# Blocks of three q tiles, products of ones and a shifted conversion table in a linear attention, MLP and MoE kernel

## The chip, the cores and the metric

The kernel runs on one core of a Trainium2 chip. The metric is device time in microseconds for one execution of the whole program, which computes an attention, an MLP and a mixture of experts one after the other.

## The reference

Cut to what is computed:

```python
# attention: q, k, v are (4, 8, 576, 64), float32
q_s = exp(q - max(q, -1)); q_s /= sum(q_s, -1) + 1e-9      # softmax over the head dimension
k_s = exp(k - max(k, 2));  k_s /= sum(k_s, 2) + 1e-9       # softmax over the sequence
out = q_s @ (k_s^T v)                                       # 2304 tokens x 512
# MLP: 512 -> 2048 -> 512
h = x @ w_in;  x = maximum(0.01 * h, h) @ w_out
# MoE: 8 experts of 512 -> 1024 -> 512, all computed, weighted by P
P = exp(x @ w_gate - max);  8 times: rows to 1, columns to 1, times N / E
out = sum_e P[:, e] * (maximum(x @ w1[e], 0) @ w2[e])
```

## The kernel before

Tokens are taken in six blocks of 384, each of three tiles of 128 tokens. The attention and the MLP are written by hand as a table of half-steps (`at(t, task)` in `plan`, run by `half_step`). Negative half-steps, -13 to -1, hold attention work alone. From half-step 0 on, the MLP runs: step s issues its first product (`first`, tile ph) and at half-step 2s + 1 its second (`second`, tiles y). The MLP's hidden units come in four phases of 24 steps; phase 0 takes blocks 0 to 2 in two passes and then block 3 (steps 12 to 15), block 4 (16 to 19) and block 5 (20 to 23). Tasks are generators: every `yield` hands over to the next half-step, and a task that has yielded PE_NEXT runs after the MLP product of its half-step instead of ahead of it. Each engine executes its instructions in the order in which this table emits them, so an instruction that waits holds all that stand behind it on its engine.

- `q_task` (line 283) makes the softmax of one tile of q in place in `acc`, a stage in each half-step: the maximum on VectorE (L291), the subtraction on GpSimd (L293), the exponential on ScalarE (L295), then sum, add and reciprocal on VectorE (L297 to L299) and the scaling on GpSimd (L300); two half-steps later come four transposes on TensorE (tile pq) and the copy back (L306).
- `k_task` (line 251) does the same for a pair of heads of k (tiles knm, ksm), with transposes (pk, L265), copies (ke, L267) and the product with v (pkv), whose two halves are scaled into `kv` (L281).
- `x_task` (line 308) multiplies the three q tiles of a block by `kv` (px), and splits the result into a rounded part (L331, ScalarE) and a rest (L332, VectorE), both in `xs`. The MLP's `first` of that block reads `xs`.
- `prep_half` (line 138) turns half a unit of the MLP's weights, loaded as 64-bit numbers (tile raw), into two float32r parts: the absolute value on ScalarE (L146), three VectorE operations a half-step later (L148, L149, L152), then the cast on ScalarE (L156) with two more on VectorE (L157, L158), and last two operations (L162, L163), on VectorE for phase 0 (tile wa) and on GpSimd for later phases. Its last stage also issues the load of another raw tile.
- PSUM banks: `bank` takes them in rotation from `spare`. Ahead of the MLP that is the pool ps_m (four buffers) and the four banks y0 to y3, which later hold the MLP's sums; line 758 adds them.
- Line 746 writes `WARM` products of ones into y0 at the start of the program.

```python
755:        (q_load, 0, 2, 3), (v_load, 0, 3), (load,), (load,),
758:    spare.extend((ps_y, f"y{i}") for i in range(4))
759:    for t in range(-R, 0):
760:        half_step(t)
729:    for t, (f, half) in zip((26, 28, 29, 32, 34, 36, 40, 42), halves):
730:        at(t, prep_half, PU + f, half)
```

Of the kernel before, what the change touches and what calls it, by code (L numbers as in the profile page):

```python
# [8 lines left out]
F32 = mybir.dt.float32  # L9
# [3 lines left out]
ALU = mybir.AluOpType  # L13
AX = mybir.AxisListType

P = 128
# [6 lines left out]
def kernel(  # L23
# [26 lines left out]
    nc = tc.nc  # L50
    B, _, HP, S = kt.shape
    NT, DM = out.shape
# [3 lines left out]
    KC = DM // P  # L56
    D = 64
    H = DM // D
    SC = vt.shape[3] // P
    TT = NT // P  # L60
    BLK = 384
    TB = BLK // P
# [15 lines left out]
    ps_y = ctx.enter_context(tc.tile_pool(name="ps_y", bufs=1, space=bass.MemoryType.PSUM))  # L78
# [1 line left out]
    att_ctx, ml_ctx = ExitStack(), ExitStack()  # L80
    later = {}
    PE_NEXT, DONE = 1, 2
    WARM = 10
    FAR = 14

    def r32(ap):
# [3 lines left out]
    ident = const.tile([P, P], F32, name="ident")  # L90
    ones = const.tile([P, P], F32, name="ones")
# [3 lines left out]
    acc = [const.tile([P, XS], F32, name=f"acc{b}") for b in range(NB)]  # L95
# [12 lines left out]
    att = att_ctx.enter_context(tc.tile_pool(name="att", bufs=2, side="right"))  # L108
# [14 lines left out]
    halves = ((0, 0), (1, 0), (0, 1), (2, 0), (1, 1), (3, 0), (2, 1), (3, 1))  # L123
# [57 lines left out]
    spare = [(ps_m, "m")]  # L181

    def bank(name):
        pool, tag = spare[0]
        spare.append(spare.pop(0))
        return pool.tile([P, 512], F32, tag=tag, name=name)

    def mm(o, a, b, start, stop, **more):
        nc.tensor.matmul(o, a, b, start=start, stop=stop, **more)  # L189

    def first(s):
        _, b, u, _, _ = steps[s]
        assert all(("x", i) in ready for i in range(b * TB, (b + 1) * TB)), (s, b)
        assert (u, 0) in ready, (s, u)
        p = bank(f"ph{s}")[:, :BLK]
        wh, wl = unit(u)[:, 0, 0, :], unit(u)[:, 0, 1, :]
        xh, xl = xb(b, 0), xb(b, 1)
        for c in range(KC):
            cs = slice(c * P, (c + 1) * P)
            mm(p, wh[:, cs], xh[:, c, :], c == 0, False)  # L200
            mm(p, wh[:, cs], xl[:, c, :], False, False)
            mm(p, wl[:, cs], xh[:, c, :], False, c == KC - 1)
        hh = h_t[s] = hp_.tile([P, 2, BLK], F32R, tag="hh", name=f"hh{s}")
        g = hp_.tile([P, BLK], F32, tag="g", name=f"g{s}", bufs=1)
        nc.scalar.activation(hh[:, 0, :], p, AF.Prelu, alpha=0.01)  # L205
        nc.scalar.activation(g, p, AF.Prelu, alpha=0.01)  # L206
        nc.vector.tensor_tensor(hh[:, 1, :], g, r32(hh[:, 0, :]), op=ALU.subtract)  # L207
# [72 lines left out]
            js = slice(j * D, (j + 1) * D)  # L280
            nc.scalar.mul(kv[b % 2][js, hp, js], pt[js, js], sm[js])  # L281

    def q_task(i):

        bl = i // TB
        o = i * P - bl * BLK
        qt = acc[bl][:, o * KC : (o + P) * KC]
        qs = qt.rearrange("p (h d) -> p h d", d=D)
        mx = att.tile([P, H, 1], F32, tag="qmx", name=f"qmx{i}", bufs=3)
        sm = att.tile([P, H, 1], F32, tag="qsm", name=f"qsm{i}", bufs=3)  # L290
        nc.vector.tensor_reduce(mx, qs, axis=AX.X, op=ALU.max)  # L291
        yield
        nc.gpsimd.tensor_tensor(qs, qs, mx.to_broadcast([P, H, D]), op=ALU.subtract)  # L293
        yield
        nc.scalar.activation(qt, qt, AF.Exp)  # L295
        yield
        nc.vector.tensor_reduce(sm, qs, axis=AX.X, op=ALU.add)  # L297
        nc.vector.tensor_scalar_add(sm, sm, EPS)
        nc.vector.reciprocal(sm, sm)  # L299
        nc.gpsimd.tensor_tensor(qs, qs, sm.to_broadcast([P, H, D]), op=ALU.mult)  # L300
        yield
        yield PE_NEXT
        pt = bank(f"pq{i}").rearrange("p (c t) -> p c t", t=P)
        for c in range(KC):
            nc.tensor.transpose(pt[:, c, :], qt[:, c * P : (c + 1) * P], ident)
        nc.scalar.copy(qt.rearrange("p (c t) -> p c t", t=P), pt)  # L306

    def x_task(bl):

# [340 lines left out]
    def at(t, f, *a):  # L650
        plan.setdefault(t, []).append((f, a))

    def advance(tasks):
        for task in tasks:
            task[1] = next(task[0], DONE)

    def half_step(t, f=None, *a):
        for g, b in plan.pop(t, ()):
            task = g(*b)
            if task is not None:  # L660
                active.append([task, None])
        now = [x for x in active if x[1] != PE_NEXT]
        then = [x for x in active if x[1] == PE_NEXT]
        advance(now)
        if f is not None:
            f(*a)
        advance(reversed(then))
        active[:] = [x for x in active if x[1] != DONE]
# [34 lines left out]
    for b, tk, tv, ts in (  # L703
# [5 lines left out]
        for hp, t in enumerate(ts):  # L709
# [1 line left out]
                at(tk[hp], k_load, b, hp)  # L711
                at(tv[hp], v_load, b, hp)
            at(t, k_task, b, hp)
    for b, tq, ts in (
        (0, None, (-12, -10, -9)), (1, -12, (-8, -7, -6)), (2, -7, (-3, -3, -2)),
        (3, 2, (8, 9, 11)), (4, 8, (13, 14, 15)), (5, 11, (16, 17, 18)),
    ):
        if tq is not None:
            at(tq, q_load, b, 0, TB)
        for j, t in enumerate(ts):  # L720
            at(t, q_task, b * TB + j)
        at(ts[-1] + 5, x_task, b)
    for t, (u, half) in zip((-12, -8, -5, -1, 3, 6, 8, 11), halves0):
        at(t, prep_half, u, half)
    at(24, lambda: nc.sync.dma_start(wg_t, wg) and None)
    at(26, open_units)
    H2 = 2 * SP

    for t, (f, half) in zip((26, 28, 29, 32, 34, 36, 40, 42), halves):
        at(t, prep_half, PU + f, half)  # L730
    for ph in range(1, NPH - 1):
        for n, (f, half) in enumerate(halves):
# [10 lines left out]

    nc.vector.memset(ones, 1.0)
    nc.scalar.activation(mrow, ones[:, :1], AF.Exp)
    warm = ps_y.tile([P, 512], F32, tag="y0", name="warm")
    for _ in range(WARM):
        mm(warm[:, :P], ones, ones, True, True)
    make_identity(nc, ident)
    for t in kv:  # L750
        nc.gpsimd.memset(t, 0.0)
    for f, *a in (
# [2 lines left out]
        (q_load, 0, 2, 3), (v_load, 0, 3), (load,), (load,),  # L755
    ):
        f(*a)
    spare.extend((ps_y, f"y{i}") for i in range(4))
    for t in range(-R, 0):
        half_step(t)  # L760
    spare[:] = [(ps_m, "m")]
    first(0)

# [9 lines left out]
    t = END  # L773
# [47 lines left out]
```

## Time and profile before

| | us |
|---|---|
| median of 3 runs | 2021.68 (2020.82 to 2025.1) |
| the profiled execution's own time | 2021.46 |
| its span, first to last instruction | 2019.6 |
| TensorE busy | 1990.9 (99%) |
| VectorE busy | 1300.8 (64%) |
| ScalarE busy | 806.7 (40%) |
| GpSimd busy | 486.5 (24%) |

The span is what the profile sees between the first and the last instruction; the execution's own time lies 1.9 us above it. Busy shares are means over stages with different limits: the MoE, which takes most of the span, is a chain of TensorE products, while the first 48 us hold attention work alone. TensorE runs at one of two clocks, 1.2 or 2.4 GHz; the profile gives the granted clock as 0.50 or 1.00.

### The profile page before, as it was taken

To read this page: it belongs to the slowest core of one execution; us is meant where nothing else is said; L and a number is where in the kernel's file an instruction comes from. 1 tells how busy PE (TensorE), PEld (TensorE's weight loads), DVE (VectorE), ACT (ScalarE), POOL (GpSimd) and SP (SyncE) were. 2 spreads that over 40 slices of the span, in tenths; PEclk is the share of its full clock that TensorE was granted. 3 is DMA by queue.
4 is the path that set the end of the run, shared out by engine and by line. 5 is a ranking of instruction groups with operands and counts; after the bars stand their busy time and mean duration, and the time that the engine had idled before them with its cause. 6 is when DMAs were issued, how large, how long until landed. Compare 5 with 4: busy or idle time off the path is not lost.

```text
span 2019.6 us, 26345 instructions
## 1 busy us (share of the span) xinstructions
PE 1990.9 (99%) x10323; PEld 1825.1 (90%) x10323; DVE 1300.8 (64%) x1953; ACT 806.7 (40%) x1367; POOL 486.5 (24%) x476
## 2 busy tenths in 40 slices
PE   7999999999999999999999999999999999999998
PEld 6999999999889999989999999999999999999997
DVE  7766435445786666666766666666686666666663
ACT  6654323234443333333444333334344333333331
POOL 3124222300223223122122231231322322313220
PEclk7999999999999999999999999999999999999999
DMA  6502111100212212212132122121212221211210
GB/s 221 175 12 81 45 43 42 53 1 1 85 43 84 84 42 84 70 56 84 42 115 84 43 84 73 54 84 48 78 68 89 84 82 44 84 55 72 84 42 32
DMA packets 65453, 138.56 MB, mean 69 GB/s; under 512 B 4656, under 2 KB 4656, under 8 KB 65328
## 3 DMA queue, kind: packets, MB, share of 16 engines
q1 hardware_dynamic: 65328, 136.87, 19.6%
q8 instruction: 81, 1.33, 0.3%
q14 instruction: 44, 0.36, 0.1%
HBM read 132.14 MB, written 4.72 MB: 68 GB/s over the span
## 4 chain that ended last, share of the span: by engine, by line
PE 73%; DVE 1%; ACT 0%; issue 0%; ACTq 0%; DVEq 0%
PE e L189 38%; PE pa L189 10%; PE pc L189 10%; PE pd L189 10%; PE pb L189 5%; DVE wa L458 0%; PE y L189 0%; DVE xs L565 0%; ACT wa L457 0%; DVE pm L399 0%; DVE cs L400 0%; PE pcs L189 0%; PE pt L189 0%; PE pg L189 0%; DVE rs L398 0%; DVE rs L396 0%
## 5 line engine op out<-in xcount | busy, mean ns | idle before, releaser
L189 PE MATMUL e<-wb_t,xs 128*128 128x512 f32 x3456 | 803.4, 390 | 0.0
L189 PEld LDWEIGHTS e<-wb_t,xs 128*128 128x128 f32 x3456 | 647.0, 188 | 131.2
L464 POOL TENSOR_TENSOR s<-pair 128x256 f32<-128x256 f32 x96 | 72.5, 755 | 1186.1 <-DMA pair<-in_w 719.3
L558 DVE SCALAR_TENSOR_TENSOR acc<-e,pm,acc 128x512 f32<-128x512 f32 x264 | 193.0, 743 | 99.5 <-PE e L189 98.3
L189 PE MATMUL pa<-xs,wa 128*128 128x384 f32 x1152 | 234.2, 337 | 0.0
L565 DVE SCALAR_TENSOR_TENSOR xs<-c,xs 128x384 fp32r<-128x384 f32 (+1 forms) x192 | 185.2, 983 | 70.9 <-ACT xs L564 70.9
L189 PE MATMUL pc<-xs,wa 128*128 128x384 f32 x1152 | 230.8, 334 | 0.0
L189 PE MATMUL pd<-xs,wa 128*128 128x384 f32 x1152 | 230.6, 334 | 0.0
L564 ACT ACTIVATE xs<-c 128x768 fp32r<-128x768 f32 x192 | 126.8, 682 | 231.8 <-PE e L189 211.1
L189 PEld LDWEIGHTS pa<-xs,wa 128*128 128x128 f32 x1152 | 204.6, 188 | 7.2
L189 PEld LDWEIGHTS pc<-xs,wa 128*128 128x128 f32 x1152 | 202.4, 188 | 0.2 <-issue 0.2
L189 PEld LDWEIGHTS pd<-xs,wa 128*128 128x128 f32 x1152 | 202.4, 188 | 0.1
L207 DVE TENSOR_TENSOR hh<-g,hh 128x384 fp32r<-128x384 f32 x96 | 58.4, 609 | 197.8 <-ACT g L206 197.8
L458 DVE TENSOR_TENSOR wa<-s,wa 128x768 fp32r<-128x768 f32 x96 | 91.8, 957 | 106.1 <-ACT wa L457 106.0
L457 ACT CAST wa<-s 128x768 fp32r<-128x768 f32 x96 | 80.2, 836 | 170.8 <-POOL s L467 150.2
L580 DVE TENSOR_TENSOR c<-c 128x384 f32<-128x384 f32 x96 | 53.9, 561 | 133.4 <-ACT c L600 133.4
L590 ACT COPY c<-pa 128x384 f32<-128x384 f32 x96 | 46.1, 480 | 198.9 <-PE pa L189 193.5
L458 DVE TENSOR_TENSOR wa<-pair,wa 128x1024 fp32r<-128x1024 f32 x96 | 120.2, 1252 | 5.2 <-ACT wa L457 5.1
L205 ACT ACTIVATE hh<-ph 128x384 fp32r<-128x384 f32 x96 | 47.3, 492 | 184.1 <-PE y L189 170.6
L458 DVE TENSOR_TENSOR wb_t<-pair,wb_t 128x1024 fp32r<-128x1024 f32 x96 | 114.1, 1223 | 7.0 <-PE y L189 3.2
L189 PE MATMUL y<-hh,wa 128*128 128x384 f32 x576 | 112.4, 344 | 4.2 <-ACT acc L226 3.6
L467 POOL TENSOR_TENSOR s<-pair,s 128x256 f32<-128x256 f32 x96 | 113.8, 1185 | 7.5
(117 smaller groups left out, 2528.7 us busy)
## 6 DMA issues: line engine op xcount, KB each, us to landing
pair<-in_w SPq DMA_DIRECT2D x192, 512.0 KB, 5.1
raw<-in_wm SPq DMA_DIRECT2D x32, 512.0 KB, 3.8
v<-in_vt SPq DMA_DIRECT2D x16, 320.0 KB, 5.8
k<-in_kt SPq DMA_DIRECT2D x16, 288.0 KB, 5.6
out<-acc SPq DMA_DIRECT2D x18, 256.0 KB, 2.0
acc<-in_q SPq DMA_DIRECT2D x5, 768.0 KB, 7.6
acc<-in_q SPq DMA_DIRECT2D x3, 256.0 KB, 6.3
wg_t<-in_wg SPq DMA_DIRECT2D x1, 16.0 KB, 3.5
```

Of the source, the lines that this page charges most:

```text
L189: nc.tensor.matmul(o, a, b, start=start, stop=stop, **more)
L205: nc.scalar.activation(hh[:, 0, :], p, AF.Prelu, alpha=0.01)
L207: nc.vector.tensor_tensor(hh[:, 1, :], g, r32(hh[:, 0, :]), op=ALU.subtract)
L457: nc.scalar.copy(hi, a)
L458: return lambda: nc.vector.tensor_tensor(lo, a, r32(hi), op=ALU.subtract)
L464: nc.gpsimd.tensor_tensor(s[:, 0], a21, a22, op=ALU.add)
L467: nc.gpsimd.tensor_tensor(s[:, 2], a12, s[:, 1], op=ALU.subtract)
L558: nc.vector.scalar_tensor_tensor(a, y, scale, a, op0=ALU.mult, op1=ALU.add)
L564: nc.scalar.activation(o[:, 0], p, AF.Relu)
L565: nc.vector.scalar_tensor_tensor(o[:, 1], p, 0.0, r32(o[:, 0]), op0=ALU.max, op1=ALU.subtract)
L580: add = lambda o, x, y: nc.vector.tensor_tensor(o, x, y, op=ALU.add)
L590: nc.scalar.copy(c1, bk[0])
```

## The change

- `q_task` takes the tiles j0 to j1 of a block. Block 0 is still taken tile by tile. Blocks 1 to 5 are one task each: one instruction of 1536 columns where there were three of 512, on VectorE, GpSimd and ScalarE; the transposes and copies stay one per tile, one in each half-step. The starts are -8, -4, 9, 13 and 16, and q_load of blocks 4 and 5 is issued a half-step earlier (7 and 10). The half-steps of `x_task` are the same as before.
- `FILL` = 4 products of ones (128x128 by 128x128, tile warm) follow each of the 13 negative half-steps. They write bank y3, which is no longer in the rotation.
- The conversions of phase 1 start at 26, 28, 32, 34, 36, 41, 43, 45 and not at 26, 28, 29, 32, 34, 36, 40, 42.

```diff
--- before.py
+++ after.py
@@ -80,7 +80,7 @@
     att_ctx, ml_ctx = ExitStack(), ExitStack()
     later = {}
     PE_NEXT, DONE = 1, 2
-    WARM = 10
+    WARM, FILL = 10, 4
     FAR = 14
 
     def r32(ap):
@@ -280,30 +280,32 @@
             js = slice(j * D, (j + 1) * D)
             nc.scalar.mul(kv[b % 2][js, hp, js], pt[js, js], sm[js])
 
-    def q_task(i):
-
-        bl = i // TB
-        o = i * P - bl * BLK
-        qt = acc[bl][:, o * KC : (o + P) * KC]
+    def q_task(bl, j0, j1):
+
+
+        n = j1 - j0
+        qt = acc[bl][:, j0 * DM : j1 * DM]
         qs = qt.rearrange("p (h d) -> p h d", d=D)
-        mx = att.tile([P, H, 1], F32, tag="qmx", name=f"qmx{i}", bufs=3)
-        sm = att.tile([P, H, 1], F32, tag="qsm", name=f"qsm{i}", bufs=3)
+        mx = att.tile([P, TB * H, 1], F32, tag="qmx", name=f"qmx{bl}_{j0}", bufs=3)[:, : n * H]
+        sm = att.tile([P, TB * H, 1], F32, tag="qsm", name=f"qsm{bl}_{j0}", bufs=3)[:, : n * H]
         nc.vector.tensor_reduce(mx, qs, axis=AX.X, op=ALU.max)
         yield
-        nc.gpsimd.tensor_tensor(qs, qs, mx.to_broadcast([P, H, D]), op=ALU.subtract)
+        nc.gpsimd.tensor_tensor(qs, qs, mx.to_broadcast([P, n * H, D]), op=ALU.subtract)
         yield
         nc.scalar.activation(qt, qt, AF.Exp)
         yield
         nc.vector.tensor_reduce(sm, qs, axis=AX.X, op=ALU.add)
         nc.vector.tensor_scalar_add(sm, sm, EPS)
         nc.vector.reciprocal(sm, sm)
-        nc.gpsimd.tensor_tensor(qs, qs, sm.to_broadcast([P, H, D]), op=ALU.mult)
-        yield
-        yield PE_NEXT
-        pt = bank(f"pq{i}").rearrange("p (c t) -> p c t", t=P)
-        for c in range(KC):
-            nc.tensor.transpose(pt[:, c, :], qt[:, c * P : (c + 1) * P], ident)
-        nc.scalar.copy(qt.rearrange("p (c t) -> p c t", t=P), pt)
+        nc.gpsimd.tensor_tensor(qs, qs, sm.to_broadcast([P, n * H, D]), op=ALU.mult)
+        yield
+        for j in range(n):
+            yield PE_NEXT
+            t = qt[:, j * DM : (j + 1) * DM]
+            pt = bank(f"pq{bl}_{j0 + j}").rearrange("p (c t) -> p c t", t=P)
+            for c in range(KC):
+                nc.tensor.transpose(pt[:, c, :], t[:, c * P : (c + 1) * P], ident)
+            nc.scalar.copy(t.rearrange("p (c t) -> p c t", t=P), pt)
 
     def x_task(bl):
 
@@ -711,22 +713,20 @@
                 at(tk[hp], k_load, b, hp)
                 at(tv[hp], v_load, b, hp)
             at(t, k_task, b, hp)
-    for b, tq, ts in (
-        (0, None, (-12, -10, -9)), (1, -12, (-8, -7, -6)), (2, -7, (-3, -3, -2)),
-        (3, 2, (8, 9, 11)), (4, 8, (13, 14, 15)), (5, 11, (16, 17, 18)),
-    ):
-        if tq is not None:
-            at(tq, q_load, b, 0, TB)
-        for j, t in enumerate(ts):
-            at(t, q_task, b * TB + j)
-        at(ts[-1] + 5, x_task, b)
+    for j, t in enumerate((-12, -10, -9)):
+        at(t, q_task, 0, j, j + 1)
+    at(-4, x_task, 0)
+    for b, tq, t in ((1, -12, -8), (2, -7, -4), (3, 2, 9), (4, 7, 13), (5, 10, 16)):
+        at(tq, q_load, b, 0, TB)
+        at(t, q_task, b, 0, TB)
+        at(t + 7, x_task, b)
     for t, (u, half) in zip((-12, -8, -5, -1, 3, 6, 8, 11), halves0):
         at(t, prep_half, u, half)
     at(24, lambda: nc.sync.dma_start(wg_t, wg) and None)
     at(26, open_units)
     H2 = 2 * SP
 
-    for t, (f, half) in zip((26, 28, 29, 32, 34, 36, 40, 42), halves):
+    for t, (f, half) in zip((26, 28, 32, 34, 36, 41, 43, 45), halves):
         at(t, prep_half, PU + f, half)
     for ph in range(1, NPH - 1):
         for n, (f, half) in enumerate(halves):
@@ -743,9 +743,13 @@
 
     nc.vector.memset(ones, 1.0)
     nc.scalar.activation(mrow, ones[:, :1], AF.Exp)
-    warm = ps_y.tile([P, 512], F32, tag="y0", name="warm")
-    for _ in range(WARM):
-        mm(warm[:, :P], ones, ones, True, True)
+    warm = ps_y.tile([P, 512], F32, tag="y3", name="warm")
+
+    def fill(n):
+        for _ in range(n):
+            mm(warm[:, :P], ones, ones, True, True)
+
+    fill(WARM)
     make_identity(nc, ident)
     for t in kv:
         nc.gpsimd.memset(t, 0.0)
@@ -755,9 +759,11 @@
         (q_load, 0, 2, 3), (v_load, 0, 3), (load,), (load,),
     ):
         f(*a)
-    spare.extend((ps_y, f"y{i}") for i in range(4))
+    spare.extend((ps_y, f"y{i}") for i in range(3))
+
     for t in range(-R, 0):
         half_step(t)
+        fill(FILL)
     spare[:] = [(ps_m, "m")]
     first(0)
 
```

VectorE, from the last k maximum ahead of the MLP to the first results of `x_task` of block 0 (qsm and qmx are the sums and maxima of q, knm the maximum of k, ca and raw the conversion's tiles, px the product of q and kv, acc_78 and acc_79 blocks 1 and 2). Before:

```order
L255 TENSOR_REDUCE knm_3_394<-k_3_285 128x1
L297 TENSOR_REDUCE qsm_342<-acc_78 128x8
L298 TENSOR_SCALAR qsm_342<-qsm_342 128x8
L299 RECIPROCAL qsm_342<-qsm_342 128x8
L157 TENSOR_SCALAR raw_1_143<-ca_1_365 128x512
L158 SCALAR_TENSOR_TENSOR raw_1_143<-raw_1_143 128x512
L291 TENSOR_REDUCE qmx_419<-acc_79 128x8
L291 TENSOR_REDUCE qmx_422<-acc_79 128x8
L332 TENSOR_TENSOR xs<-px_0_425,xs 128x384
L332 TENSOR_TENSOR xs<-px_1_429,xs 128x384
```

The change:

```order
L255 TENSOR_REDUCE knm_3_416<-k_3_309 128x1
L291 TENSOR_REDUCE qmx_0_419<-acc_79 128x24
L157 TENSOR_SCALAR raw_1_143<-ca_1_388 128x512
L158 SCALAR_TENSOR_TENSOR raw_1_143<-raw_1_143 128x512
L334 TENSOR_TENSOR xs<-px_0_445,xs 128x384
L334 TENSOR_TENSOR xs<-px_1_449,xs 128x384
```

The last sum of block 1 has moved ahead, into one wide sum (which stands just ahead of L162 and L163 of the conversion before), and the maximum of block 2, now one instruction of three tiles, stands ahead of L157 and L158 and no longer behind them.

TensorE, the last products ahead of the MLP's first one (ph), from the second half of block 0's px on. Before:

```order
L189 MATMUL px_2_460<-acc_77,kv_96 128x384
L189 MATMUL px_3_464<-acc_77,kv_96 128x384
L265 MATMUL pk_3_0_469<-ident,k_3_285 128x128 x4
L265 MATMUL pk_3_4_475<-ident,k_3_285 64x128
L189 MATMUL pkv_2_480<-v_2_283,ke_2_433 128x128 x5
L305 MATMUL pq_488<-ident,acc_78 128x128 x4
L189 MATMUL pkv_3_499<-v_3_329,ke_3_468 128x128 x5
L305 MATMUL pq_507<-ident,acc_78 128x128 x4
L189 MATMUL ph_513<-xs,wa 128x384 x12
```

The change:

```order
L307 MATMUL pq_0_465<-ident,acc_78 128x128 x4
L189 MATMUL warm<-ones 128x128 x4
L189 MATMUL px_2_480<-acc_77,kv_96 128x384
L189 MATMUL px_3_484<-acc_77,kv_96 128x384
L265 MATMUL pk_3_0_489<-ident,k_3_309 128x128 x4
L265 MATMUL pk_3_4_495<-ident,k_3_309 64x128
L189 MATMUL pkv_2_500<-v_2_307,ke_2_453 128x128 x5
L307 MATMUL pq_1_508<-ident,acc_78 128x128 x4
L189 MATMUL warm<-ones 128x128 x4
L189 MATMUL pkv_3_524<-v_3_354,ke_3_488 128x128 x5
L307 MATMUL pq_2_532<-ident,acc_78 128x128 x4
L189 MATMUL warm<-ones 128x128 x4
```

The transposes of block 1's first tile (pq_0) keep their place ahead of px_2; three groups of products of ones now stand between the attention's products here, the last directly ahead of ph.

ScalarE around the copies of the MLP's sums out of PSUM (acc_80 is block 3, acc_82 block 5; L156 is a conversion's cast). Before, block 3:

```order
L156 CAST wb_t<-ca_0_1572 128x512
L205 ACTIVATE hh_1650<-ph_1637 128x384
L206 ACTIVATE g_1651<-ph_1637 128x384
L156 CAST wb_t<-ca_1_1617 128x512
L226 COPY acc_80<-y_12_1505 128x384
```

The change, block 3:

```order
L206 ACTIVATE g_1568<-ph_1554 128x384
L156 CAST wb_t<-ca_0_1534 128x512
L205 ACTIVATE hh_1607<-ph_1594 128x384
L206 ACTIVATE g_1608<-ph_1594 128x384
L226 COPY acc_80<-y_12_1467 128x384
```

The change, block 5:

```order
L146 ACTIVATE ca_1_1898<-raw_1_1778 128x512
L205 ACTIVATE hh_1932<-ph_1919 128x384
L206 ACTIVATE g_1933<-ph_1919 128x384
L156 CAST wb_t<-ca_1_1898 128x512
L226 COPY acc_82<-y_20_1816 128x384
```

Ahead of block 3's copies the last cast has gone; ahead of block 5's, where the last operations before were those of the MLP, a cast now stands.

## Rows read from the trace of the kernel before

**Rows 1.** The page: the span, and TensorE's busy time.

```profile
span 2019.6 us, 26345 instructions
...
PE 1990.9 (99%) x10323; PEld 1825.1 (90%) x10323; DVE 1300.8 (64%) x1953; ACT 806.7 (40%) x1367; POOL 486.5 (24%) x476
```

**Rows 2.** Windows by clock: stretch, its us, busy of each engine, PEclk, DMA.

```profile
8.24:15.07 6.83, 5.66 (x24) 5.14 (x25) 6.66 (x15) 5.77 (x15) 1.15 (x1) 0.50 1.05 417
...
21.90:42.38 20.48, 17.14 (x60) 13.13 (x60) 19.83 (x39) 14.07 (x35) 10.13 (x9) 0.50 0.37 134
42.38:62.85 20.47, 18.03 (x117) 16.57 (x118) 15.05 (x32) 11.04 (x24) 5.68 (x6) 1.00 0.36 124
62.85:66.27 3.42, 3.42 (x15) 3.41 (x14) 1.56 (x4) 2.93 (x6) 0.00 (x0) 0.50 0.42 108
```

**Rows 3.** VectorE's timeline: start, us, operation, idle time before it and releaser.

```profile
19.26 0.75 DVE L255 TENSOR_REDUCE knm<-k 128x1 f32<-128x576 f32 x1 [1.45 <-DMA k<-in_kt]
...
24.23 1.42 DVE L152 SCALAR_TENSOR_TENSOR ca<-raw,ca 128x512 uint32<-128x512 uint32 x1
...
32.15 1.41 DVE L163 TENSOR_TENSOR wa<-ca,raw 128x512 fp32r<-128x512 f32 x1
...
35.84 1.15 DVE L149 TENSOR_SCALAR ca<-ca 128x512 uint32<-128x512 uint32 x1
37.02 0.69 DVE L152 SCALAR_TENSOR_TENSOR ca<-raw,ca 128x512 uint32<-128x512 uint32 x1
...
38.29 0.68 DVE L297 TENSOR_REDUCE qsm<-acc 128x8 f32<-128x512 f32 x1
...
39.33 0.38 DVE L157 TENSOR_SCALAR raw<-ca 128x512 uint32<-128x512 uint32 x1
39.74 1.41 DVE L158 SCALAR_TENSOR_TENSOR raw<-raw 128x512 f32<-128x512 uint32 x1
41.07 1.26 DVE L291 TENSOR_REDUCE qmx<-acc 128x8 f32<-128x512 f32 x2
42.26 1.00 DVE L332 TENSOR_TENSOR xs<-px,xs 128x384 fp32r<-128x384 f32 x2
...
51.93 0.56 DVE L207 TENSOR_TENSOR hh<-g,hh 128x384 fp32r<-128x384 f32 x1 [5.00 <-ACT g L206]
```

**Rows 4.** GpSimd's timeline in the same stretch.

```profile
23.88 1.22 POOL L293 TENSOR_TENSOR acc<-acc,qmx 128x512 f32<-128x512 f32 x1
...
39.56 1.05 POOL L300 TENSOR_TENSOR acc<-acc,qsm 128x512 f32<-128x512 f32 x1 [2.85 <-DVE qsm L299]
```

**Rows 5.** Timelines of GpSimd and of VectorE in the second phase's conversions.

```profile
179.82 1.51 POOL L163 TENSOR_TENSOR wb_t<-ca,raw 128x512 fp32r<-128x512 f32 x1
...
180.08 1.52 DVE L148 TENSOR_SCALAR ca<-ca 128x512 f32<-128x512 f32 x1
```

**Rows 6.** TensorE's timeline, from the first products to the MLP's third.

```profile
1.05 4.29 PE L189 MATMUL warm<-ones 128*128 128x128 f32 x20 [1.05 <-DVE ones L744]
...
42.86 1.56 PE L189 MATMUL px<-acc,kv 128*128 128x384 f32 x4 [0.73 <-DVE xs L332]
...
46.35 0.63 PE L305 MATMUL pq<-ident,acc 128*128 128x128 f32 x4
46.81 1.50 PE L189 MATMUL pkv<-v,ke 128*128 128x128 f32 x10
...
48.65 4.41 PE L189 MATMUL ph<-xs,wa 128*128 128x384 f32 x24
...
61.88 1.18 PE L189 MATMUL ph<-xs,wa 128*128 128x384 f32 x5 [1.88 <-DVE xs L332]
```

**Rows 7.** Timelines of TensorE and of VectorE at 103 to 108 us.

```profile
103.88 2.37 PE L189 MATMUL ph<-xs,wa 128*128 128x384 f32 x12 [1.03 <-ACT ke L267]
...
107.36 1.42 DVE L163 TENSOR_TENSOR wa<-ca,raw 128x512 fp32r<-128x512 f32 x1
```

**Rows 8.** Timelines of ScalarE and TensorE around the sums of blocks 3 and 4.

```profile
165.50 0.62 ACT L156 CAST wb_t<-ca 128x512 fp32r<-128x512 f32 x1 [2.75 <-DVE ca L152]
...
166.55 2.39 PE L189 MATMUL y<-hh,wa 128*128 128x384 f32 x12 [2.62 <-ACT acc L226]
...
184.64 2.38 PE L189 MATMUL y<-hh,wa 128*128 128x384 f32 x12 [1.01 <-ACT acc L226]
```

## The prediction

> **What bounds the kernel now.** I read the page first: a span of 2019.6 us of which TensorE is busy for 1990.9 [rows 1]. At most 29 us are not TensorE work, and the change touches nothing of the MoE, so I looked only at the first 200 us. The windows by clock come second [rows 2]: three stretches, of 6.83, 20.48 and 3.42 us, ran at a granted clock of 0.50 (1.2 GHz), the rest at 1.00 (2.4 GHz). Third, the timelines. VectorE starts an operation at 19.26 us, after a wait for a load of k, and its next idle time is the 5.00 us ahead of 51.93 [rows 3]; it is 19.83 of 20.48 us busy while TensorE's clock is low [rows 2]. So from 19 us to the first results of x_task (42.26) the bound is VectorE's queue, not TensorE and not its clock. Behind that, TensorE's own queue sets the end: from 42.86 to the MLP's first product at 48.65 it has no gap worth naming [rows 6]. From then on TensorE's order decides, with single stops: 1.88 us ahead of 61.88 [rows 6], 1.03 us ahead of 103.88 [rows 7], 2.62 and 1.01 us behind the copies of blocks 3 and 4 [rows 8].
>
> One more thing has to be seen in VectorE's rows. The same operation takes two durations: L152 0.69 us at 37.02, but 1.42 at 24.23; L163 1.41; L158 1.41; L149 1.15 [rows 3]. Each long one starts within 0.4 us of the start of a GpSimd operation (23.88, 39.56) [rows 4] and ends after it. In the second phase L148 takes 1.52 us at 180.08, where GpSimd began a 1.51 us operation at 179.82 [rows 5]: VectorE stood until GpSimd had finished. The maxima and sums (L291, L297) show no second duration.
>
> **The change, part by part.** Sums are made against the profiled execution's own 2021.46 us, 0.2 us below the median of the three runs.
>
> **q by blocks, VectorE.** A GpSimd operation of 512 columns takes 1.05 us [rows 4]; one of 1536 is estimated at three times that, 3.14, so it lasts 2.09 us longer. Before the results at 42.26 VectorE now stands behind GpSimd six times, about 0.72 us each (1.41 less 0.69; four are in [rows 3], two more are like them). In the new order three of these places meet a wide operation: L152 the subtraction of block 1, L163 the scaling of block 1, L158 the subtraction of block 2. Two stay as they are behind operations of block 0, which is still taken by tiles; the one at 35.84 goes, as no GpSimd operation starts there any more. I take the long ones at their full excess: 3 x 2.09 - 0.72 = +5.5 us. VectorE's own work: a tile's sum, add and reciprocal take 1.04 us (38.29 to 39.33 [rows 3]), three of them 3.12. The wide version saves two sets of small operations: about 0.9 us, estimated from the 0.44 us by which 1.04 exceeds a maximum's pace of 0.60 (41.07 to 42.26 for two [rows 3]). Against that, the third maximum of block 2 moves ahead of 42.26: +0.6. Together **+5.2 us** at the first results of x_task.
>
> The Trainium skill, SBUF — State Buffer, section "Who interferes with whom", says that VectorE and GpSimd share a port pair under an exclusive lock, held for the whole instruction, which `tensor_scalar` and operations with two SBUF inputs meet and `tensor_reduce` does not. The trace agrees for operations of up to 1.51 us; no run here shows one of 3.14. By that rule the sum is mine; if instead a wait could grow no longer than the rows have shown, the change would come out faster (the first rival).
>
> **Products of ones.** Ten took 4.29 us at the low clock for most of the time [rows 6], so four cost 1.7 us there and about 0.9 at the high one. Those between 19 and 42 us lie beside VectorE's queue: TensorE's 17.14 us at the low clock [rows 2] are some 9 at the high one, and six groups add 5. Were the cover gone (the low clock throughout), 10 us would meet 3.3 free ones. The groups ahead of 19 us lie where loads set the pace (VectorE waits for one until 19.26 [rows 3]). Three groups stand on the path, behind px_2: **+2.6 us**. With y3 taken out of the rotation there are four places and no longer five, so the first transposes of block 1, ahead of px_2, now wait for the first results of x_task as well, where before they were done: +0.5 (0.46 from 46.35 to 46.81 [rows 6]). The first MLP product thus comes 5.2 + 2.6 + 0.5 = 8.3 us later, at about 57 us.
>
> **Behind it.** The last sums of block 2 no longer stand between the MLP's first operations and its third product: the 1.88 us go, and so does the slow stretch of 3.42 us that followed, which gives back half, 1.7. Together **-3.6**. A fall of the clock in another gap would take the 1.7 back; I take 0 and keep 1.7 for the range.
>
> **Blocks 3 and 4.** At 103 to 108 us TensorE stops for 1.03 us behind a ke copy, which stood in ScalarE's queue behind a conversion that waited for VectorE [rows 7]. Two wide GpSimd operations fall there, the scaling of block 3 (against L149) and the subtraction of block 4 (against L162). Bounds: 0, if a half-step of lead covers both, and 2 x 2.8 = 5.6, if each whole wait gets through. The 1.03 us say that there is no lead left, so I take 2 x 2.09 less the 1.03: **+3.2**.
>
> **Conversions.** The copies of block 3 wait for the cast of a conversion that began two half-steps earlier (29, copies at 31): 2.62 us [rows 8]. With its start at 32 that goes. Block 4 keeps its conversion at 36, three half-steps ahead of the copies at 39, and its 1.01 us. But 45 is two half-steps ahead of 47, the copies of block 5: the same 2.62 again. **0**, between -2.6 and +1. Issuing q_load for blocks 4 and 5 a half-step earlier costs SyncE one issue and moves nothing that waits.
>
> **Sum:** 8.3 - 3.6 + 3.2 = +7.9, so **2029.4 us**.
>
> **The rivals.** *Faster: a wide operation holds VectorE no longer than a narrow one.* Five long waits carry the sum: with x us of excess each, it is 5x - 2.5. At x = 2.09 that is +7.9; it changes sign at x = 0.5. At x = 0, and if block 5's copies happen to meet no late cast (-2.6), it is -5.1: 2016.3 us. For it: only 1.05 and 1.51 us operations have been seen. Against it: in both, VectorE waited to the end.
>
> *Faster: TensorE's clock is the bound.* The three slow stretches hold 26.2 us of TensorE work [rows 2]; at the high clock half of it, 13.1, would come back: 2008.4. Against it stands VectorE without idle time through the longest stretch. The Trainium skill, TensorE: Matmul & The Clock Gate, Part 1, has the clock follow how busy TensorE has been, and by it the products of ones do raise the clock; that agrees with the low clock after the idle times here, and says nothing about who waits for TensorE.
>
> *No change that can be told.* The wide operations cost what I say ahead of the MLP (8.3 - 3.6 = +4.7), but blocks 3 and 4 have cover, and block 5 meets no late cast (-2.6): +2.1, 2023.6. For it: VectorE is idle for 5.4 of the 20.5 us behind 42.38 [rows 2], so that it has lead to give.
>
> *Slower still.* The clock stays low through the groups of ones on the path, and each whole wait reaches TensorE: 7.9 + 1.7 + 2.4 = +12, 2033.5, or a little over if the cover of the groups is gone too.
>
> **How the numbers follow.** A measurement of this kernel tells 0.2%, 4 us, from no change. The forecast has 0.57, the slower case 0.10 (both are slower by over 4 us), no change 0.20, the first faster rival 0.10, the second 0.03. Faster 0.13, same 0.20, slower 0.67. The range reaches from 2018, which leaves out the faster rivals (0.13), to 2034.5 (some 0.05 above). The forecast's own range is 2025.7 to 2034.
>
> **What would show it.** Right: three VectorE operations of over 3 us between 24 and 48 us, each beside a GpSimd operation of about 3.1; the MLP's first product near 57 us; no stop ahead of its third; a longer stop near 110 to 120 us; the stop behind block 3's copies gone and one behind block 5's. Wrong: VectorE's operations never above 1.5 us beside wide GpSimd ones; the first product of the MLP earlier than 50 us; TensorE without stops from 100 to 200 us.

## The result, and the profile after

The changed kernel takes 2032.53 us (2032.13 to 2033.99, 4 runs) beside 2021.74 us (2020.82 to 2025.1, 4 runs) of the kernel before on the same chip: a ratio of 1.0056, 95% interval 1.0044 to 1.0068, so 8.9 to 13.7 us slower. The forecast was 7.9 us slower: 2029.4 us, with a range up to 2034.5.

Two lines of the page, against [rows 1]. TensorE has 104 matmul records more: 13 groups of four products of ones, two records each.

```profile
span 2031.0 us, 26462 instructions
...
PE 2001.2 (99%) x10427; PEld 1835.6 (90%) x10427; DVE 1307.8 (64%) x1913; ACT 804.7 (40%) x1357; POOL 481.6 (24%) x456
```

**Where the time comes in** is read from marks: the start of TensorE's first product (tile ph) of an MLP step, here and in each run of the next section, less the same mark of the kernel before (48.65, 67.80, 151.21, 172.98 and 259.35 us). A stop is idle time of TensorE ahead of an instruction, a slow stretch one in which its granted clock is 0.50. Step 0 closes the attention's front, step 15 the stage of blocks 3 and 4, step 20 stands behind block 3's copies, step 40 behind block 5's; from there to the end of the MLP nothing changes any more.

| kernel | step 0 | step 3 | step 15 | step 20 | step 40 | ratio to before, 95% interval |
|---|---|---|---|---|---|---|
| changed | +8.9 | +5.1 | +12.0 | +9.1 | +11.3 | 1.0056 (1.0044 to 1.0068) |
| e1_split | +4.1 | +0.3 | +3.1 | +0.3 | +2.5 | 1.0015 (1.0005 to 1.0024) |
| e2_nofill | +6.5 | +2.7 | +8.2 | +5.3 | +7.6 | 1.0047 (1.0030 to 1.0064) |
| e3_oldconv | +10.0 | +6.2 | +12.9 | +14.3 | +14.4 | 1.0064 (1.0049 to 1.0079) |
| e4_bytile | +6.7 | +6.6 | +6.6 | +3.7 | +5.9 | 1.0032 (1.0017 to 1.0047) |
| s_blk | +6.1 | +2.3 | +7.9 | +7.9 | +7.9 | 1.0031 (1.0021 to 1.0042) |
| s_fill | +5.7 | +5.7 | +5.7 | +5.7 | +5.8 | 1.0028 (1.0017 to 1.0040) |
| s_bank | +3.9 | +3.9 | +3.9 | +3.9 | +3.9 | 1.0004 (0.9994 to 1.0013) |
| s_conv | -0.3 | -1.9 | -1.9 | -4.8 | -1.0 | 1.0002 (0.9993 to 1.0011) |
| e5_later | +10.6 | +6.8 | +7.6 | +4.7 | +6.9 | 1.0029 (1.0019 to 1.0038) |
| e6_front | +10.1 | +6.3 | +6.3 | +3.4 | +5.7 | 1.0028 (1.0018 to 1.0037) |
| s_c3 | -0.1 | -1.8 | -1.8 | -4.7 | -5.9 | 0.9977 (0.9968 to 0.9987) |
| mix | +1.3 | -2.5 | -2.4 | -5.3 | -6.6 | 0.9966 (0.9955 to 0.9978) |

The marks are those of one profiled execution each. How far one trace can be trusted is seen in step 0 of the changed kernel, e3, e5 and e6: up to there these are the same program, and they stand at +8.9, +10.0, +10.6 and +10.1. Nor do the -1.9 and -1.8 at step 3 in s_conv and s_c3 come from their edits, which lie behind it: the stop ahead of the third product is there as before (1.89 us), but in these two executions no slow stretch follows it.

**The front.** VectorE's timeline of the changed kernel, against [rows 3]:

```profile
24.41 1.15 DVE L149 TENSOR_SCALAR ca<-ca 128x512 uint32<-128x512 uint32 x1
25.59 3.13 DVE L152 SCALAR_TENSOR_TENSOR ca<-raw,ca 128x512 uint32<-128x512 uint32 x1
...
31.00 1.42 DVE L158 SCALAR_TENSOR_TENSOR raw<-raw 128x512 f32<-128x512 uint32 x1
...
35.21 3.13 DVE L163 TENSOR_TENSOR wa<-ca,raw 128x512 fp32r<-128x512 f32 x1
...
43.46 3.13 DVE L158 SCALAR_TENSOR_TENSOR raw<-raw 128x512 f32<-128x512 uint32 x1
46.51 1.01 DVE L334 TENSOR_TENSOR xs<-px,xs 128x384 fp32r<-128x384 f32 x2
```

and GpSimd's, against [rows 4]:

```profile
25.24 2.94 POOL L293 TENSOR_TENSOR acc<-acc,qmx 128x1536 f32<-128x1536 f32 x1
...
34.77 3.02 POOL L300 TENSOR_TENSOR acc<-acc,qsm 128x1536 f32<-128x1536 f32 x1 [2.90 <-DVE qsm L299]
43.17 2.87 POOL L293 TENSOR_TENSOR acc<-acc,qmx 128x1536 f32<-128x1536 f32 x1 [5.38 <-DVE qmx L291]
```

The three operations of over 3 us are there: each starts 0.3 to 0.4 us behind a 1536-column operation of GpSimd and ends 0.5 us behind its end. Those beside a 512-column operation last 1.15 and 1.42 us, as before. The first results of x_task are made at 46.51, and were at 42.26.

TensorE's timeline, against [rows 6]:

```profile
41.14 2.35 PE L189 MATMUL px<-acc,kv 128*128 128x384 f32 x4 [3.58 <-ACT acc L308]
...
47.20 0.63 PE L307 MATMUL pq<-ident,acc 128*128 128x128 f32 x4 [2.65 <-DVE xs L334]
47.67 1.06 PE L189 MATMUL warm<-ones 128*128 128x128 f32 x8
48.56 2.73 PE L189 MATMUL px<-acc,kv 128*128 128x384 f32 x4
...
53.98 1.06 PE L189 MATMUL warm<-ones 128*128 128x128 f32 x8
...
56.77 1.06 PE L189 MATMUL warm<-ones 128*128 128x128 f32 x8
57.58 4.41 PE L189 MATMUL ph<-xs,wa 128*128 128x384 f32 x24
...
67.51 0.60 PE L307 MATMUL pq<-ident,acc 128*128 128x128 f32 x4
67.87 2.33 PE L189 MATMUL ph<-xs,wa 128*128 128x384 f32 x12
```

TensorE waits longer than before, not shorter: 3.58 and 2.65 us, each for what VectorE's queue holds up. The px wait is for a copy on ScalarE, whose queue, by the times, waited for a maximum of k that stands on VectorE behind the long L163. The pq wait ends with the first results of x_task, which set a PSUM place free. Three groups of ones stand on the way to 57.58, some 0.9 us each. Ahead of the third product at 67.87 nothing stops any more.

The windows by clock, against [rows 2] (the granted clock is the third number from the end):

```profile
8.24:21.29 13.05, 9.43 (x70) 8.19 (x69) 11.37 (x24) 8.44 (x22) 4.23 (x4) 1.00 1.03 386
21.29:42.38 21.09, 15.48 (x87) 13.40 (x88) 20.58 (x30) 12.78 (x29) 8.74 (x5) 0.82 0.39 143
42.38:62.85 20.47, 17.82 (x106) 14.89 (x105) 12.01 (x20) 10.16 (x23) 5.63 (x2) 0.85 0.36 124
116.86:123.69 6.83, 6.18 (x23) 5.92 (x23) 5.47 (x12) 1.58 (x3) 0.00 (x0) 0.50 0.29 79
```

The products of ones did what they say: 1.00 where 8.24 to 15.07 had 0.50, and a mean of 0.82 where the kernel before had 0.50 nearly throughout. It paid nothing, since VectorE is busy for 20.58 of the 21.09 us. The fourth line is a slow stretch that the kernel before does not have.

**The stage of blocks 3 and 4.** TensorE's timeline and then VectorE's, against [rows 7]:

```profile
110.66 0.77 PE L265 MATMUL pk<-ident,k 128*128 128x128 f32 x5 [0.96 <-ACT ke L267]
...
113.67 0.63 PE L307 MATMUL pq<-ident,acc 128*128 128x128 f32 x4 [0.74 <-ACT g L206]
...
117.51 3.57 PE L189 MATMUL y<-hh,wa 128*128 128x384 f32 x10 [2.85 <-DVE wa L163]
```

```profile
104.97 2.87 DVE L149 TENSOR_SCALAR ca<-ca 128x512 uint32<-128x512 uint32 x1
...
113.52 3.21 DVE L162 TENSOR_TENSOR ca<-ca,wa 128x512 f32<-128x512 f32 x1
116.76 0.69 DVE L163 TENSOR_TENSOR wa<-ca,raw 128x512 fp32r<-128x512 f32 x1
```

L149 stands behind the scaling of block 3, L162 behind the subtraction of block 4, on GpSimd:

```profile
104.80 2.76 POOL L300 TENSOR_TENSOR acc<-acc,qsm 128x1536 f32<-128x1536 f32 x1 [6.49 <-ACT hh L205]
113.42 2.76 POOL L293 TENSOR_TENSOR acc<-acc,qmx 128x1536 f32<-128x1536 f32 x1 [5.85 <-DVE ksm L268]
```

The ends of both reach TensorE, the second as 2.85 us ahead of a y product, and the clock falls in that stop, at 116.86.

**The conversions.** TensorE's single stops behind 150 us, against [rows 8]:

```profile
193.71 2.38 PE L189 MATMUL y<-hh,wa 128*128 128x384 f32 x12 [1.01 <-ACT acc L226]
...
212.72 2.39 PE L189 MATMUL y<-hh,wb_t 128*128 128x384 f32 x12 [1.94 <-ACT acc L226]
```

Block 3's 2.62 us are gone, block 4's 1.01 us have stayed, and block 5 has a stop of 1.94 us.

### The profile page after: what moved, and what is told of

The parts are those of the page before. It is cut to its first block, busy times and chain, and to the rows that moved or that the text cites. A ratio compares the mean times of both kernels' runs of the same rounds, so it can differ in the third digit from the quotient of the medians.

```text
span 2031.0 us, 26462 instructions
## 1 busy us (share of the span) xinstructions
PE 2001.2 (99%) x10427; PEld 1835.6 (90%) x10427; DVE 1307.8 (64%) x1913; ACT 804.7 (40%) x1357; POOL 481.6 (24%) x456
## 4 chain that ended last, share of the span: by engine, by line
PE 73%; DVE 1%; ACT 0%; issue 0%; ACTq 0%; DVEq 0%
PE e L189 38%; PE pa L189 10%; PE pc L189 10%; PE pd L189 10%; PE pb L189 5%; PE y L189 0%; DVE wa L460 0%; DVE xs L567 0%; ACT wa L459 0%; DVE pm L401 0%; DVE cs L402 0%; PE pcs L189 0%; PE pt L189 0%; PE pg L189 0%; DVE rs L400 0%; DVE rs L398 0%
```

## The experiments

**Each part taken out of the changed kernel.** First the length of GpSimd's instructions, with all else whole (the same is done to L300):

```diff
-        nc.gpsimd.tensor_tensor(qs, qs, mx.to_broadcast([P, n * H, D]), op=ALU.subtract)
+        for j in range(n):
+            t, m = (x[:, j * H : (j + 1) * H] for x in (qs, mx))
+            nc.gpsimd.tensor_tensor(t, t, m.to_broadcast([P, H, D]), op=ALU.subtract)
```

> GpSimd's subtraction and scaling of a block in three instructions of 512 columns each; all else as in the change. Theory (a wide GpSimd operation holds VectorE to its end): the three VectorE operations of 3.13 us at 25.6, 35.2 and 43.5 us fall back to about 1.4, the first MLP product comes some 5 us earlier (52.5 and not 57.6), the stop of 2.8 us at the copies of block 0's sums goes, in all 7 to 10 us: 2022.5 to 2025.5. Rival 1 (the products of ones and the missing bank set the time): nothing moves, 2032.5. Rival 2 (whole-block tasks are late as such, since the transposes wait for all three tiles): nothing moves either.

Measured: 2023.57 us. The same columns by the same engine, and 8.8 of the 11.3 us (marks at step 40) are gone. GpSimd's timeline, and VectorE's beside it:

```profile
33.57 3.98 POOL L304 TENSOR_TENSOR acc<-acc,qsm 128x512 f32<-128x512 f32 x3 [2.91 <-DVE qsm L301]
```

```profile
34.00 1.41 DVE L163 TENSOR_TENSOR wa<-ca,raw 128x512 fp32r<-128x512 f32 x1
```

Three pieces need 3.98 us where one instruction needed 3.02, and yet VectorE's L163, which starts beside them, lasts 1.41 us and not 3.13: it gets in behind the first piece. What holds VectorE is the length of one instruction, not the work. At the stage of blocks 3 and 4, 2.9 of the 6.8 us are left, a stop of 1.86 us at the same place with a slow stretch of 3.4 us behind it.

Then the products, `WARM, FILL = 10, 0`, with y3 still out of the rotation:

> FILL = 0, bank y3 still out of the rotation; all else as in the change. Theory: only the three groups behind px_2 were on the path, 0.9 us each, so the first MLP product comes 2 to 2.6 us earlier; behind it nothing moves: 2029.9 to 2030.5. If TensorE's clock mattered ahead of the MLP, leaving the products out would make it slower: above 2032.5. Rival 1 (the products of ones set the time): 2026 or less.

Measured: 2029.84 us. At step 0 it is 2.4 us ahead of the changed kernel, about the three groups on the path (the medians differ by 2.7); another 1.3 us come from the stage of blocks 3 and 4, where this execution's slow stretch is half as long (116.24 to 119.65 us).

Then the conversions at the half-steps of before:

> The conversions of phase 1 at their old half-steps; all else as in the change. Theory: the stop behind block 3's copies comes back (2.6 us less what the trace of the change still has), the one behind block 5's (1.9 us) goes: 0.5 to 1 us slower, 2033.2. Rival (the new table is worth its 2.9 us, or costs its 2.2 us): 2035.4 or 2030.3.

Measured: 2033.65 us, not to be told from the changed kernel. The marks rise at block 3 (step 20), where in this execution a slow stretch of 3.41 us follows the stop of 2.62, and no longer at block 5.

Then q by tiles at the half-steps of before, with products, places and conversions as changed:

> q by tiles at the old half-steps; products of ones and new conversions stay. Theory: with the wide operations 8 to 10 us go; the first MLP product comes at about 52 us (the groups on the path and the missing bank stay), the 1.9 us ahead of its third product come back: 2022 to 2025. Rival 1 (products of ones, bank): still 2028 or more.

Measured: 2027.67 us, 2.7 us above the interval expected: step 0 is at +6.7, where the prediction's terms give +3.1. The stage of blocks 3 and 4 adds nothing (+6.6 at steps 3 and 15). The miss opened a question: do the products or the missing place cost more than the prediction has it? The next runs take the parts alone.

**Each part added alone to the kernel before.** The blocks, with the table and `q_task` of the change and nothing else of it:

> The kernel before with q by blocks alone (no products of ones, the fifth bank back, the conversions as before). If the wide operations are the loss, it keeps nearly all of what was left without the products (8.1 us over before): 5 to 6.5 us at the MLP's first product, the 1.88 us stop ahead of its third gone, 4 to 7 us more at the blocks 3 and 4 stage, block 3's 2.62 us stop still there and none at block 5: 2028 to 2031 us. If instead the wide operations cost only together with the missing bank or the products, it is below 2025 us.

Measured: 2027.14 us; the marks are those expected (+6.1, +2.3, then +7.9 to the end), the time lies 1 us under the interval given.

The products and four places, nothing else:

> The kernel before with the products of ones and four places in place of five, and nothing else. By the prediction's terms (2.6 of products on the path, 0.5 of the place): 3.1 us at the first MLP product, at most that at the end, 2024 to 2025 us. If what the run with q by tiles showed (6.7 us at the first MLP product) belongs to the products and the place and not to a chance of that order: 6 to 7 us at the first MLP product and 2027 to 2029 us.

and four places without any product (`FILL = 0`):

> As the run with the products of ones alone, but none are issued ahead of the MLP's half-steps: only the fifth place is taken out of the rotation. By the prediction 0.5 us at the first MLP product: 2021 to 2023 us. If the missing place is what costs with q by tiles (TensorE's products wait for a bank, and that holds the order up): 3 to 5 us at the first MLP product, 2024 to 2027 us; the run with the products then stands only 2 to 3 us above it.

Measured: 2026.84 and 2022.12 us. The place alone costs 0.8 us by its ratio (0.9994 to 1.0013), which is not to be told from nothing nor from the 0.5 predicted; the profiled execution of that run was the slowest of its ten, at 2025.38, and its +3.9 is not typical. The products with q by tiles cost the rest, nearly 5 us, more than the 2.7 by which the changed kernel's median stands over that of e2, with q by blocks. What TensorE's timeline shows of it, first with the products, then without:

```profile
43.03 1.08 PE L307 MATMUL pq<-ident,acc 128*128 128x128 f32 x4 [3.73 <-POOL acc L293]
43.91 1.91 PE L189 MATMUL warm<-ones 128*128 128x128 f32 x8
45.62 2.76 PE L189 MATMUL px<-acc,kv 128*128 128x384 f32 x4
```

```profile
43.56 1.09 PE L307 MATMUL pq<-ident,acc 128*128 128x128 f32 x4 [1.62 <-POOL acc L293]
```

The GpSimd operation named had long been done; the wait ends where the first results of x_task do (L334, 42.39 us and 0.56 long), so it is for a place. With the faster clock TensorE comes to this wait earlier and stands in it for 3.73 us, 1.62 in the run without products; the clock falls there (0.50 from 41.68 to 48.51), and the group of ones takes 1.7 us and not 0.9, px 2.76 and not 1.56 [rows 6]. In this execution, then, the products spent their faster clock on a wait. That the low clock behind it comes of the products is not shown: the profiled execution without them has it too (0.50 from 32.55 to 49.61, px 2.77 us).

The conversion times alone:

> The kernel before with the new conversion times alone. The 2.62 us stop at block 3 goes and one of 2.2 to 2.6 us comes at block 5: by the prediction 0, by the changed kernel's marks (2.9 less, then 2.2 more) 0.7 us below before: 2020.5 to 2021.7 us. Rival: half-steps moved apart also lengthen or shorten the blocks' ways ahead of 150 us; then the difference stands already at the MLP's step of block 3.

Measured: 2022.82 us, ratio 0.9993 to 1.0011. The marks lose 2.9 us at block 3 and gain 3.8 at block 5, where 1.93 us of stop are followed by a slow stretch of 3.41 us (the same stop in the changed kernel is followed by none, and costs 2.2):

```profile
198.83 3.10 PE L189 MATMUL y<-hh,wb_t 128*128 128x384 f32 x12 [1.93 <-ACT acc L226]
```

The three parts alone sum to 6.3 + 5.7 + 0.4 = 12.4 us by their ratios, against 11.3 (8.9 to 13.7) together: most of the loss needs no interplay of the parts. A few us either way would not show in this sum, and the products did cost less with q by blocks (2.7) than with q by tiles (4.7).

**The stage of blocks 3 and 4.** One run moves the collision away:

```diff
-    for b, tq, t in ((1, -12, -8), (2, -7, -4), (3, 2, 9), (4, 7, 13), (5, 10, 16)):
+    for b, tq, t in ((1, -12, -8), (2, -7, -4), (3, 2, 9), (4, 7, 14), (5, 10, 17)):
```

> The changed kernel with blocks 4 and 5 started a half-step later (14 and 17 for 13 and 16, their x_task with them), nothing else. If the stage of blocks 3 and 4 costs because VectorE's L162 starts beside block 4's 1536-column subtraction and holds the y product (2.85 us, and 0.74 us ahead of it) with the slow clock that follows: these stops go, the 0.96 us one behind block 3's scaling stays, and the end comes 3.5 to 6 us earlier than the changed kernel's: 2026.5 to 2029 us. Rival: whole blocks load VectorE there whatever half-step they start at; the stop only moves: 2031 to 2034 us.

Measured: 2026.25 us, though its front was 1.7 us later than the changed kernel's. VectorE's timeline and TensorE's:

```profile
106.63 2.87 DVE L149 TENSOR_SCALAR ca<-ca 128x512 uint32<-128x512 uint32 x1
...
113.51 0.67 DVE L162 TENSOR_TENSOR ca<-ca,wa 128x512 f32<-128x512 f32 x1
114.22 0.69 DVE L163 TENSOR_TENSOR wa<-ca,raw 128x512 fp32r<-128x512 f32 x1
```

```profile
112.32 0.77 PE L265 MATMUL pk<-ident,k 128*128 128x128 f32 x5 [0.96 <-ACT ke L267]
...
115.33 0.63 PE L307 MATMUL pq<-ident,acc 128*128 128x128 f32 x4 [0.74 <-ACT g L206]
115.71 2.37 PE L189 MATMUL y<-hh,wa 128*128 128x384 f32 x12
```

L162 takes 0.67 us, the 2.85 us stop and the slow stretch are gone, and the stage adds 0.8 us and not 6.8. The 0.74 us ahead of pq stayed, against the expectation: by its releaser it waits for ScalarE's g, and so, it seems, for a queue that stands behind L149's chain and not L162's.

The other run has blocks 1 and 2 whole and blocks 3 to 5 by tiles, as in the kernel before:

> The changed kernel with blocks 1 and 2 whole, and blocks 3 to 5 by tiles at the half-steps of the kernel before; products and conversions as changed. If the stage's 6.8 us is made there, the MLP's step behind it stands no later against before than step 3 does (5.1 us), and the end is at 4.5 to 6 us over before: 2026 to 2028 us. Rival: it is the front's lateness that uses up the lead of the stage; then half of the 6.8 or more stays: above 2029.5 us.

Measured: 2027.46 us; step 3 and step 15 both at +6.3. The stage's loss is made in the stage, and a late front alone brings none.

**Versions that might beat both.** The kernel before with only the start times of its conversions changed, to 26, 28, 30, 33, 35, 38, 41, 43:

> The kernel before with the conversions at 26, 28, 30, 33, 35, 38, 41, 43, and nothing else: none starts two half-steps ahead of the copies of blocks 3, 4 and 5 (31, 39, 47), and the nearest ones, at 30 and 38, come so late that their casts should stand behind the copies. If the distance of a cast to the copies is what counts, the stops of 2.62 and 1.01 us go and none comes: 3 to 4 us less, 2017.5 to 2018.5 us. Rival: the casts at 30 and 38 get ahead of the copies and hold them as before: 2020.5 to 2023 us.

Measured: 2016.73 us, ratio 0.9968 to 0.9987, so 4.6 us less by the ratio. Of the 5.9 us at step 40, 2.9 are block 3's and 1.25 block 4's; most of the rest is the slow stretch that this execution lacks at step 3. ScalarE's timeline at block 3, before and here:

```profile
166.03 1.62 ACT L226 COPY acc<-y 128x384 f32<-128x384 f32 x4
```

```profile
158.92 0.62 ACT L156 CAST wb_t<-ca 128x512 fp32r<-128x512 f32 x1 [2.15 <-DVE ca L152]
160.85 1.64 ACT L226 COPY acc<-y 128x384 f32<-128x384 f32 x4
164.35 0.62 ACT L156 CAST wb_t<-ca 128x512 fp32r<-128x512 f32 x1 [1.87 <-DVE ca L152]
```

The copies stand with 1.3 us of room behind one cast and 1.9 us ahead of the next, where before, at 166.03, they followed the late cast of 165.50 at once [rows 8]; from 150 to 215 us TensorE has no stop left.

Last, that together with the blocks used only where they help: blocks 1 and 2 whole on VectorE and ScalarE with GpSimd by tiles, blocks 3 to 5 by tiles, no products, five places, the second conversion at 27.

> What the runs so far speak for, put together: blocks 1 and 2 whole on VectorE and ScalarE but with GpSimd's operations by tiles, blocks 3 to 5 by tiles as before, no products of ones, five places, conversions at 26, 27, 30, 33, 35, 38, 41, 43. Front: the 4.05 us of the run with split operations less 2.8 of the products and the place, +1.2; the stop ahead of the third product and its slow clock, -3.8; the stage of blocks 3 and 4, 0; conversions -3.6. Sum -6.2: 2015 us, between 2013 and 2018. If it is at 2020 or above, what the parts give back alone does not come together.

Measured: 2014.25 us (2013.39 to 2017.28, 8 runs), ratio 0.9955 to 0.9978: by the ratio 6.9 us under the kernel before, and faster than both kernels. TensorE's timeline at the MLP's start:

```profile
49.99 4.41 PE L189 MATMUL ph<-xs,wa 128*128 128x384 f32 x24
...
60.28 2.33 PE L189 MATMUL ph<-xs,wa 128*128 128x384 f32 x12
```

The MLP begins 1.3 us later than before, but its third product at 60.28 meets no stop.

## Why the prediction was right, and what was mis-sized

Sign, mechanism and range held. By its own steps, with the changed kernel's marks:

- **VectorE behind wide operations, +5.2.** Measured +4.25 (46.51 for 42.26). GpSimd's wide operations took 2.87 to 3.02 us and not the estimated 3.14, so the excess is 3.13 less 1.41 = 1.72 us and not 2.09: 3 x 1.72 - 0.72 - 0.3 = 4.1. (One reading is a little off: L163 at 32.15 starts 0.45 us behind its GpSimd operation, not within 0.4.) The Trainium skill, SBUF — State Buffer, section "Who interferes with whom", has the lock last for the whole instruction of the other engine; that agrees up to 3.02 us here, and e1_split shows that it is given up between instructions.
- **Products +2.6 and place +0.5.** Between the first results of x_task and the MLP lie 11.07 us, 6.39 before: +4.7. Of it some 3.1 are groups of ones and the transposes ahead of px, as predicted, and 1.6 are px and pk at the slow clock (px 2.73 for 1.56, pk 1.16 for 0.71), which were not in the sum. e2_nofill gives 2.4 for the products, s_bank 0.8 for the place. Front: +8.9, forecast +8.3; that these are so close is in part luck, since VectorE's term came out 0.95 too large and the slow clock was left out.
- **Behind it, -3.6.** Measured -3.8; both the stop and the slow stretch went. The 1.7 us of the slow stretch hang on the execution compared with: of the six traces that have this stop, four have the slow stretch behind it, and s_conv and s_c3 do not.
- **Blocks 3 and 4, +3.2.** Measured +6.8: this is the term that was mis-sized. Its stops were right: 0.96 + 0.74 + 2.85 less the 1.03 of before is 3.5. What was wrong is the step "A fall of the clock in another gap would take the 1.7 back; I take 0". The clock fell behind this very stop, for 6.83 us with 6.18 us of TensorE's work, of which half, 3.1, is lost: 3.5 + 3.1 = 6.6. e5_later removes stop and slow stretch together. How long the slow stretch is differs: all four traces with the 2.85 us stop have one, of 6.83 us here and in e3, of 3.41 in e2 and s_blk. Behind other stops it often stays away: one of five traces has it behind block 3's 2.62 us (e3), one of seven behind block 5's 1.93 or 1.94 (s_conv). What decides it is open.
- **Conversions, 0.** Marks -2.9 and +2.2; the times of s_conv and e3 show no difference. The reasoning itself, that a cast whose conversion begins two half-steps ahead of the copies is in their way, holds: used in s_c3, it gave a gain that the change did not have.

Of the rivals, that a wide operation holds no longer than a narrow one is refuted by the 3.13 us rows, and that TensorE's clock is the bound by the windows: the clock rose and the time with it. "No change that can be told" fell with the stops of blocks 3 and 4, which had no cover, and with the stop at block 5. The slower rival, 2033.5, came closer to the result than the forecast, for one of its two reasons: the slow clock (though it fell on px, pk and behind the stop of block 4, and not on the groups of ones), not longer waits.

## What to carry to other kernels

Merging instructions saves overhead on their own engine, but where two engines hold each other for whole instructions, the length of one is a price that the other pays: widen the reductions that nobody is held by, and keep the operations of the sharing engine short, or start them where the other has no such work queued. When a stop on TensorE is forecast, price in the same sentence a clock that falls behind it, as a second case: behind one stop here it cost as much as the stop, behind others it fell in some executions and not in the rest. Work put in to keep a clock up paid nothing here, where another engine was the bound: it became longer waiting and one more thing on the path.

## What was not expected of the hardware

In the changed kernel a GpSimd operation of 1536 columns takes 2.87 to 3.02 us in the front and 2.76 or 2.77 behind it (why they differ was not tried), less than three of 512, which take 1.05 each and 3.98 together beside VectorE's L163 in e1_split.

A reduction and a wide operation leave each other alone: in the changed kernel the 1536-column maximum at 124.05 lasts 1.70 us while GpSimd works from 124.28 to 127.05, and 1.75 at 111.60 with GpSimd idle, and GpSimd's 2.77 us are no longer than elsewhere. The maximum started first here; no trace has a reduction that starts while a wide operation runs.

```profile
111.60 1.75 DVE L291 TENSOR_REDUCE qmx<-acc 128x24 f32<-128x1536 f32 x1
...
124.05 1.70 DVE L291 TENSOR_REDUCE qmx<-acc 128x24 f32<-128x1536 f32 x1
```

```profile
124.28 2.77 POOL L300 TENSOR_TENSOR acc<-acc,qsm 128x1536 f32<-128x1536 f32 x1 [8.09 <-DVE qsm L299]
...
139.12 2.76 POOL L300 TENSOR_TENSOR acc<-acc,qsm 128x1536 f32<-128x1536 f32 x1 [9.36 <-DVE qsm L299]
```

Nor does a wide operation hold every VectorE operation with two inputs. L228, which adds the MLP's sums out of PSUM to `acc`, runs four times from 138.90 on, 0.49 to 0.55 us each, and three of these start inside the GpSimd operation of 139.12; the operations that were held read both inputs from SBUF, or are a `tensor_scalar` of 512 columns (L149).

How often the clock falls in the front differs from one execution to the next of the same instructions: between 39 and 54 us it is low for two times 3.41 us in the changed kernel, and for 13.65 us without a break in e3, e5 and e6. The MLP's first product differs by up to 1.7 us, of which up to 0.6 is there already at the first results of x_task. What decides it was not tried.
